# Out-projection of the last four token tiles by seven products per pair of blocks

## The chip, the core and the metric

The kernel runs on one core of one Trainium2 chip. The metric is the device time of one execution in microseconds (us). The engines are named as the profile names them: PE (matrix multiply), PEld (its weight loads), DVE (VectorE), ACT (ScalarE), POOL (GpSimd), SP (SyncE, which here only issues DMAs). Line numbers such as L800 are those of the kernel before; where the changed kernel is meant, the text says so.

## What is computed

Linear attention with a decay per head over 4 batches, 8 heads, 768 tokens and 64 channels a head, then a feed-forward part with a gate that is the cosine of the hidden value itself. Inputs and output are float32.

```python
for b in range(nb):                       # blocks of 64 tokens, per batch and head
    intra = (qb @ kb.T * Dmask) @ vb
    out[b] = intra + (qb * lam_pow) @ kv_state
    kv_state = lam_block * kv_state + (kb * rev_pow).T @ vb
x = out as (3072 tokens, 512)
h = x @ w_in                              # 512 x 2048
g = h * cos(h)
y = g @ w_out                             # 2048 x 512
```

## The kernel before

The 3072 tokens are 24 blocks of 128. `TILES = [4, 2, 2, 2, 2, 4, 4, 4]` groups the blocks into eight tiles of the feed-forward part. Attention works on pairs of blocks (pair `pr` is blocks 2 pr and 2 pr + 1 of the order of `where`).

**Attention.** q, k and v of a pair are loaded by SP (L260). From pair 3 on POOL prepares them (`qk` L351 and L355, `v_s` L359: two q, two k, two v a pair), and SP transposes `qk` by DMA (`qkT`, L387). The load of q of the next pair is queued behind these transposes, so the loads of a pair wait, over SP, for POOL's work on the pair before. An attention part on PE is values of pair `pr` (L491), scores of pair `pr + 1` (L429), its state update (L441), then the carried part of pair `pr` (L491, L523). Ahead of the carried part PE waits for a tiny DVE copy (`spare`, L508), here called the marker. DVE masks the scores (`s_m`, L434) and adds up the state (`sum`, L447); ACT casts the state (`S`, L451) and copies the result into `xT` (L531; L540 to L548 for two of the pairs).

**Hidden part.** For each of 16 slices f of 128 columns of `w_in`, four matmuls (one per quarter of 512 channels) write one PSUM bank `ps_h` (L753); ACT takes the cosine into `cos` (L759), DVE multiplies into `g` (L765, the gate). In tiles of two blocks a matmul has 256 columns, in tiles of four 512.

**Out-projection.** For each block, 16 matmuls of 512 columns accumulate `g` times `w_out_sb` in one bank `ps_f` (L800). ACT copies the bank to `o_sb` (L816), SP stores it (L823, L825). The very last block is split into 384 and 128 columns, whose second part ACT copies and stores.

**What sets the order.** A planner (`Planner.order`) runs a list schedule over tasks with costs written by hand and emits each engine's instructions in the order of the planned starts. An engine then goes through its own list strictly; what it waits for is set by the data. PE is filled with out-projection matmuls of the tile before while attention and hidden matmuls have to wait. `HELD = (10,) * 12` holds the stores of the first twelve blocks back until the transposes of pair 10 are issued. Buffers go round by tag (`BUFS`): `o_held` has 12 buffers, taken in turn by the early q and k of the first blocks, by four slices of `w_out` that are loaded plainly (`w_f`) and by the outputs.

```python
h = pl.add("PE", MM(n, 4), ..., hidden, pr, banks=1)
a = pl.add("ACT", 0.21 + n * 0.000833, [h], cosine, pr, get="cos")
d = pl.add("DVE", 0.12 + n * 0.00104, [a] + ..., gated, pr)
```

## Time and profile before

| what | before |
|---|---|
| median of 3 runs | 202.6 us (202.12 to 202.65) |
| profiled execution, first to last instruction | 200.7 us |
| clock granted to PE | 1.000 |
| instructions | 5731 |
| out-projection matmuls (L800) in the trace | 380, of 400 weight loads |
| hidden matmuls (L753) in the trace | 525, of 532 weight loads |
| DMA traffic | 34.46 MB, mean 172 GB/s |

The profiled execution leaves a span, from its first to its last instruction, and no separate device time; the runs' median is 1.9 us above it. A matmul's own duration in a row is its latency through a pipeline; its pace is found by dividing the length of a run of them by their count. Groups of rows read: line, engine, operation, output and inputs, shapes, count, then busy us, mean ns, and idle time before them with what ended it. A row of a timeline has start and length in us. In rows of the chain of waits the length is the part of the chain that the group holds. Rows of the windows have the stretch, its length, then for PE, PEld, DVE, ACT and POOL the busy us and the number of instructions, then PE's clock, DMA share and GB/s.

### The profile page before, as it was taken

The numbers are of one execution on the slowest core, as the hardware profiler recorded it, in microseconds if no ns is written. First come the engines' busy times: TensorE is split into PE (matmuls) and PEld (weight loads), VectorE is DVE, ScalarE is ACT, GpSimd is POOL, SyncE is SP. The second block draws the span as 40 slices with busy tenths as digits, with TensorE's granted clock in tenths as the row PEclk, the third lists the DMA queues.
The fourth block names the chain that finished last, engine by engine and source line by source line (L and its number), as shares of the span: only waits on it lengthen the run. The fifth ranks groups of instructions, "written<-read, shape, count | busy, mean of one in ns | idle before, by whom it ended". The sixth has DMA issues, their size and how long they took to land.

```text
span 200.7 us, 5731 instructions
## 1 busy us (share of the span) xinstructions
PE 192.9 (96%) x2380; PEld 110.2 (55%) x2407; DVE 112.1 (56%) x211; ACT 117.1 (58%) x223; POOL 64.9 (32%) x86
## 2 busy tenths in 40 slices
PE   8899999999999999999999999999999999999993
PEld 2466444648758647858755454544445444444452
DVE  2978772448848816956745679565445453444001
ACT  5878771329769527939555878486356465344120
POOL 5893002284373645472636570006400000000000
DMA  5999999999899999998999997999611010111112
GB/s 163 303 191 202 205 196 239 289 221 177 203 218 214 184 241 201 214 213 184 191 207 220 245 206 183 318 314 223 162 56 54 3 52 6 49 52 52 52 63 97
DMA packets 96668, 34.46 MB, mean 172 GB/s; under 512 B 84738, under 2 KB 93186, under 8 KB 96642
## 3 DMA queue, kind: packets, MB, share of 16 engines
q1 hardware_dynamic: 89664, 29.83, 66.6%
q0 software_dynamic: 6832, 4.20, 14.5%
q8 instruction: 19, 0.31, 0.7%
q10 hardware_dynamic: 146, 0.07, 0.1%
q14 instruction: 7, 0.06, 0.1%
HBM read 27.26 MB, written 6.29 MB: 167 GB/s over the span
## 4 chain that ended last, share of the span: by engine, by line
PE 89%; DMA 6%; issue 1%; SPq 1%; POOL 1%; ACT 0%; POOLq 0%
PE ps_f L800 41%; PE ps_h L753 41%; DMA sp_f<-in_k_dram 3%; DMA w_in_sb<-in_moe_w_in_dram 3%; PE ps_o L491 2%; PE ps_o L523 2%; PE ps_kv L441 2%; PE ps_s L429 1%; SPq L260 1%; POOL k_sp L614 1%; PE ps_t L381 0%; PE ps_kv L718 0%; PE ps_x L491 0%; ACT o_sb L816 0%; POOLq L614 0%
## 5 line engine op out<-in xcount | busy, mean ns | idle before, releaser
L765 DVE TENSOR_TENSOR g<-ps_h,cos 128x256 bf16<-128x256 f32 (+1 forms) x133 | 70.6, 543 | 41.4 <-ACT cos L759 39.7
L800 PE MATMUL ps_f<-w_out_sb,g 128*128 128x512 bf16 (+2 forms) x380 | 87.6, 370 | 2.2 <-issue 1.6
L753 PE MATMUL ps_h<-xT,w_in_sb 128*128 128x256 bf16 (+1 forms) x525 | 88.8, 319 | 0.5 <-issue 0.2
L759 ACT ACTIVATE cos<-ps_h,halfpi 128x256 f32<-128x256 f32 (+1 forms) x133 | 72.0, 570 | 28.9 <-PE ps_h L753 28.3
L753 PEld LDWEIGHTS <-w_in_sb 128*128 128x128 bf16 x532 | 51.4, 98 | 32.9 <-DMA w_in_sb<-in_moe_w_in_dram 0.4
L800 PEld LDWEIGHTS <-g 128*128 128x128 bf16 x400 | 37.6, 98 | 40.4
L351 POOL TENSOR_TENSOR qk<-q_f,q_scale 128x512 bf16<-128x512 f32 x19 | 19.4, 1042 | 54.2 <-DMA q_f<-in_q_dram 54.2
L816 ACT COPY o_sb<-ps_f 128x512 f32<-128x512 f32 (+1 forms) x24 | 13.7, 574 | 22.6 <-PE ps_f L800 19.6
L359 POOL TENSOR_TENSOR v_s<-v_f,v_scale 128x512 bf16<-128x512 f32 x19 | 19.6, 1043 | 9.2 <-DMA v_f<-in_v_dram 5.4
L531 ACT CAST xT<-ps_o 128x512 bf16<-128x512 f32 x15 | 8.1, 589 | 13.6 <-PE ps_o L523 11.2
L434 DVE TENSOR_TENSOR s_m<-ps_s,mask 128x512 bf16<-128x512 f32 x20 | 12.9, 685 | 2.5 <-PE ps_s L429 2.0
L355 POOL CAST qk<-k_f 128x512 bf16<-128x512 f32 x18 | 11.0, 612 | 7.8 <-DMA k_f<-in_k_dram 7.8
L447 DVE TENSOR_TENSOR sum<-sum,ps_kv 128x512 f32<-128x512 f32 x15 | 10.2, 682 | 0.7
L451 ACT CAST S<-sum 128x512 bf16<-128x512 f32 x15 | 9.1, 618 | 1.0 <-DVE sum L447 0.9
L508 DVE COPY spare<-ps_o 1x1 f32<-1x1 f32 x8 | 1.2, 156 | 14.6 <-PE ps_o L491 14.6
L816 DVE COPY o_sb<-ps_f 128x384 f32<-128x384 f32 x1 | 0.6, 558 | 11.6 <-PE ps_f L800 11.6
L491 PEld LDWEIGHTS <-v_s 64*64 64x64 bf16 x320 | 4.2, 106 | 4.4 <-issue 4.0
L491 PE MATMUL ps_o<-s_m,v_s 64*64 64x64 bf16 x288 | 5.9, 197 | 0.0
L638 DVE TENSOR_TENSOR s_m_sp<-ps_s,mask_sp 128x512 bf16<-128x512 f32 x8 | 5.1, 685 | 1.3 <-PE ps_s L633 1.3
L892 PE MATMUL ps_idle<-const-float32-1.0 128*128 128x512 f32 (+1 forms) x6 | 4.8, 902 | 0.8 <-PEq L954 0.8
L523 PE MATMUL ps_o<-qkT,S 64*64 64x64 bf16 x304 | 5.0, 195 | 0.0
L441 PE MATMUL ps_kv<-v_s,qk 64*64 64x64 bf16 x288 | 4.8, 195 | 0.0
(77 smaller groups left out, 83.9 us busy)
## 6 DMA issues: line engine op xcount, KB each, us to landing
q_f<-in_q_dram SPq DMA_DIRECT2D x20, 256.0 KB, 3.9
k_f<-in_k_dram SPq DMA_DIRECT2D x20, 256.0 KB, 4.5
v_f<-in_v_dram SPq DMA_DIRECT2D x20, 256.0 KB, 4.5
out_dram<-o_sb SPq DMA_DIRECT2D x19, 256.0 KB, 2.8
w_out_sb<-in_moe_w_out_dram POOLq DMA_DIRECT2D x3, 512.0 KB, 13.6
sp_f<-in_q_dram SPq DMA_DIRECT2D x2, 512.0 KB, 4.9
sp_f<-in_k_dram SPq DMA_DIRECT2D x2, 512.0 KB, 5.4
w_in_sb<-in_moe_w_in_dram POOLq DMA_DIRECT2D x2, 512.0 KB, 9.1
```

Of the source, the lines that this page charges most:

```text
L351: return vec[e].tensor_mul(new_qk()[:, 0, :, s], live.pop(("q_f", 2 * pr + s)), q_scale[:, c, :].unsqueeze(2).to_broadcast([P, H, D]))
L355: return (nc.scalar.copy if early else nc.gpsimd.tensor_copy)(new_qk()[:, 1, :, s], live.pop(("k_f", 2 * pr + s)))
L359: return vec[e].tensor_mul(live["v_s", 2 * pr + s], live.pop(("v_f", 2 * pr + s)), v_scale[:, c, :].unsqueeze(2).to_broadcast([P, H, D]))
L434: return nc.vector.tensor_mul(t, live["s", pr][s], mask.unsqueeze(1).to_broadcast([P, H, D]))
L447: return nc.vector.tensor_add(new, live["sum", pr, 0] if half else live["sum", pr - 1, 1], live["kv", pr][half])
L451: return nc.scalar.copy(new_S(pr, half), live["sum", pr, half])
L491: yield lambda h=h: nc.tensor.matmul(o[halves[h % 2], h // 2], lhsT=live["v_s", n0 + s][m, h, :], rhs=live["s_m", n0 + s][m, h, :], start= ...
L753: return [nc.tensor.matmul(t[:, :n], lhsT=w_in_sb[:, kd, f * P:(f + 1) * P], rhs=live["xT", i][:, kd, at], start=(kd == 0), stop=(kd == KD ...
L759: nc.scalar.activation(c[:, :n], live["h", i, f, at.start][:, :n], AF.Sin, bias=halfpi)
L765: return nc.vector.tensor_mul(live["g", i][:, f, at], live.pop(("h", i, f, at.start))[:, :n], live.pop(("c", i, f, at.start))[:, :n])
L800: return [nc.tensor.matmul(live["f", i, j, piece][:, :width], lhsT=live["g", i][:, f, j * P:(j + 1) * P], rhs=w_out_sb[:, f, part], start= ...
L816: return (nc.scalar.copy if eng == "ACT" else nc.vector.tensor_copy)(o[:, :width], live["f", i, j, piece][:, :width])
```

## The change

**Seven products.** In tiles 4 to 7 (`FAST`, 2, 4, 4 and 4 blocks) the out-projection takes two blocks at a time. The two blocks are the rows of a 2 x 2 block matrix A, the halves of the 2048 hidden columns its columns; `w_out` is a 2 x 2 block matrix B of halves of rows and of columns. Strassen's scheme forms the four quarters of the result from seven products instead of eight. A product is 8 matmuls of 256 columns, in two groups (g) of four. On the left stand sums of quarters of `g`: 5, 2 and 1 are new tiles `cmb`, 7 and 6 overwrite quarters of `g`, 3 and 4 use `g` as it is. DVE forms them (ten instructions a tile, five for each g; each has 512 elements in tile 4 and 1024 in the others, both operands bf16 in SBUF). On the right stand sums of quarters of `w_out`, formed once: three new tiles by six DVE instructions, and two sums written in place into `w_out_sb` by four POOL instructions, after the last plain projection. The in-place sums belong to products 6 and 7.

Products 5 and 2 fill a bank A, 1 a bank B, 3 and 4 a bank C. ACT copies A to `SA`, DVE forms `E` = B - A in two halves and the first outputs o1 = C + A; then 7 and 6 are added onto C and DVE forms the second outputs o2 = C + E. So product 7 has to wait for o1. Each output tile goes to two stores of 256 columns. The last pair's o2 is formed in two halves, the last of which ACT stores.

**Slices that share a bank.** In tiles of two blocks, slices f and f + 8 write the halves of one bank, so ACT and DVE work on 512 columns eight times instead of 256 sixteen times. Tiles of four take their slices in the order 0, 8, 1, 9 and so on.

**Homes.** The buffers are laid out anew: 4 instead of 6 for each of q, k and v, one tag `o` of 11 buffers for all outputs, new tags for `cmb`, `SA` and `E`; the early scores and values share their space with the three weight sums. The planner frees an engine a little earlier (`TAIL`).

```diff
+FAST = [4, 5, 6, 7]
+WSUM = [["DVE"] * 3 + ["POOL"] * 2, ["DVE"] * 3 + ["POOL"] * 2]
+SEQ = [[(n, (g,)) for g, x in enumerate(("52341", "34521")) for n in x] + [(n, (0, 1)) for n in "76"], [(n, (0, 1)) for n in "5234176"]]
...
+    TAIL = {"ACT": 0.1, "DVE": 0.09, "POOL": 0.05}
...
-            free[t.eng] = t.end
+            free[t.eng] = t.end - self.TAIL.get(t.eng, 0.0)
...
-    BUFS = {"ld": 6, "qk": 3, "v_s": 6, "qkT": 3, "s_m": 4, "cos": 3, "o_sb": 3, "o_held": 12}
+    BUFS = {"ld": 4, "qk": 3, "v_s": 6, "qkT": 3, "s_m": 4, "cos": 3, "o": 11, "cmb": 2, "SA": 2, "E": 2}
...
-    span_v = [consts.tile([P, H, 2, D], BF16, name=f"v_sp{x}") for x in range(SPANS)]
+    span_s = [consts.tile([P, 2, NP, 2, P], BF16, tag="wide", bufs=3, name=f"s_m_sp{x}") for x in range(SPANS)]
+    span_vs = consts.tile([P, SPANS, H, 2, D], BF16, tag="wide", bufs=3, name="v_sp")
+    span_v = [span_vs[:, x] for x in range(SPANS)]
...
+    def add_w_sums():
+        low, high = slice(0, HM), slice(HM, DM)
+        def fresh(name):
+            if name not in W:
+                W[name] = consts.tile([P, HF, HM], BF16, tag="wide", bufs=3, name=f"w_{name}")
+            return W[name]
+        def two(_, name, g, e):
+            f, z = slice(QF * g, QF * g + QF), slice(HF + QF * g, HF + QF * g + QF)
+            b11, b12, b21, b22 = (w_out_sb[:, x, y] for x in (f, z) for y in (low, high))
+            v = nc.vector if e == "DVE" else nc.gpsimd
+            if name == "11+22":
+                return v.tensor_add(fresh(name)[:, f], b11, b22)
+            if name == "12-22":
+                return v.tensor_sub(fresh(name)[:, f], b12, b22)
+            if name == "21-11":
+                return v.tensor_sub(fresh(name)[:, f], b21, b11)
+            if name == "11+12":
+                return v.tensor_add(b12, b11, b12)
+            return v.tensor_add(b21, b21, b22)
+        on = {"DVE": 0.69, "POOL": 2.1}
+        for g in range(2):
+            loaded = [w_t["out", 0], w_t["out", 2]] if g == 0 else [w_t["out", 1]] + w_last
+            for k, name in enumerate(("11+22", "12-22", "21-11")):
+                e = WSUM[g][k]
+                w_sum[name, g] = [pl.add(e, on[e], loaded + (wide_free if name == "21-11" else []), partial(two, name=name, g=g, e=e), begins[FAST[0]] + 3.0 + 2.0 * g + 0.4 * k)]
+        for g in range(2):
+            for k, (name, others) in enumerate((("11+12", ("12-22",)), ("21+22", ("21-11",)))):
+                e = WSUM[g][3 + k]
+                w_sum[name, g] = [pl.add(e, on[e], [closed[0]] + [t for o in others for t in w_sum[o, g]], partial(two, name=name, g=g, e=e), begins[FAST[0] + 1] + 0.4 * k + 0.2 * g)]
+    def held(n):
+        return [T[HELD[n], 1].issue] if n < len(HELD) else []
...
+        if i == 0:
+            groups = [([f], b, (f + b[0] / 4 * SPLIT) / KF) for f in range(KF) for b in ([(0, 2), (2, 4)] if f < SPLIT else [(0, nb)])]
+        elif nb == 4:
+            groups = [([f], (0, nb), (2 * (f % HF) + f // HF) / KF) for x in range(HF) for f in (x, x + HF)]
+        else:
+            groups = [([x, x + HF], (0, nb), 2 * x / KF) for x in range(HF)]
+        for fs, (b0, b1), frac in groups:
+            pr = begins[i] + frac * unit[i]
+            at = slice(b0 * P, b1 * P)
+            n = (b1 - b0) * P
+            k, key = len(fs), (i, fs[0], b0)
...
+            def hidden(task, fs=fs, at=at, n=n, key=key):
+                t = bank(task.bank[0], [P, 4 * P], F32, "ps_h")
+                live["h", key] = t
+                return [nc.tensor.matmul(t[:, x * n:(x + 1) * n], lhsT=w_in_sb[:, kd, f * P:(f + 1) * P],
+                                         rhs=live["xT", i][:, kd, at], start=(kd == 0), stop=(kd == KD - 1))
+                        for x, f in enumerate(fs) for kd in range(KD)]
...
-            cuts = [0, 3 * DM // 4, DM] if last else [0, DM]
...
+            for f0, nf in [(0, 4), (4, 4), (8, 4), (12, 2), (14, 2)] if i == 0 else [(0, 4), (8, 4), (4, 4), (12, 4)]:
...
+        def combine(_, name, g):
+            a11, a12, a21, a22 = (side(x, y, g) for x in range(2) for y in range(2))
+            if ("cmb", i, g) not in live:
+                live["cmb", i, g] = work.tile([P, 3, QF, np_, P], BF16, tag="cmb", bufs=BUFS["cmb"], name="cmb")
+            c = live["cmb", i, g]
+            if name == "5":
+                return nc.vector.tensor_add(c[:, P5], a11, a12)
+            if name == "2":
+                return nc.vector.tensor_add(c[:, P2], a21, a22)
+            if name == "1":
+                return nc.vector.tensor_add(c[:, P1], a11, a22)
+            if name == "7":
+                return nc.vector.tensor_sub(a12, a12, a22)
+            return nc.vector.tensor_sub(a21, a21, a11)
+        for g in range(2):
+            ready = [t for f in range(QF * g, QF * g + QF) for t in gate[f] + gate[f + HF]]
+            head = None
+            for k, name in enumerate("52176"):
+                t = pl.add("DVE", 0.15 + np_ * QF * P / 1920.0, ready + ([head] if head else []), partial(combine, name=name, g=g),
+                           begins[i] + (0.55 + 0.06 * k + 0.45 * g) * unit[i], get=None if head else "cmb")
+                head = head or t
+                sums[name, g] = [t]
+            sums["head", g] = head
+            sums["3", g] = sums["4", g] = ready
...
+        plan_of = {"5": ("A", 0, "22"), "2": ("A", 1, "11"), "1": ("B", 0, "11+22"), "3": ("C", 0, "12-22"),
+                   "4": ("C", 1, "21-11"), "7": ("C", 1, "21+22"), "6": ("C", 0, "11+12")}
+        def left(name, f, p):
+            j = 2 * p
+            own = lambda x, y: live["g", i][:, f + HF * y, (j + x) * P:(j + x + 1) * P]
+            if name in "125":
+                return live["cmb", i, f // QF][:, {"1": P1, "2": P2, "5": P5}[name], f % QF, p]
+            return own(*{"3": (0, 0), "4": (1, 1), "6": (1, 0), "7": (0, 1)}[name])
...
+            for name, gs in SEQ[min(p, 1)]:
+                to, half, what = plan_of[name]
+                for g in gs:
+                    k += 1
+                    def product(task, name=name, g=g, p=p, to=to, half=half, what=what):
+                        if (name, g) in (("5", 0), ("1", 0), ("3", 0)):
+                            live["f", i, p, to] = bank(task.bank[0], [P, 2, HM], F32, "ps_f")
+                        t = live["f", i, p, to][:, half]
+                        return [nc.tensor.matmul(t, lhsT=left(name, f, p), rhs=right(what, f),
+                                                 start=(f == 0 and name in "513"), stop=(f == HF - 1), skip_group_check=True)
+                                for f in range(QF * g, QF * g + QF)]
+                    opens = (name, g) in (("5", 0), ("1", 0), ("3", 0))
+                    t = pl.add("PE", MM(HM, QF), sums[name, g] + w_sum.get((what, g), []) + [before] + ([done["o1"]] if name == "7" else []) + ([passed.get("4")] if (name, g) == ("5", 0) else []) + ([passed.get("6")] if (name, g) == ("3", 0) else []),
+                               product, begins[i + 1] + (p + k / 14) * nxt / np_, banks=1 if opens else 0)
...
+                if "sa" not in done and full("5") and full("2"):
+                    def copy_out(_, p=p):
+                        live["SA", i, p] = work.tile([P, 2, HM], F32, tag="SA", bufs=BUFS["SA"], name="SA")
+                        return nc.scalar.copy(live["SA", i, p], live["f", i, p, "A"])
+                    done["sa"] = pl.add("ACT", 0.6, [done["5"], done["2"]], copy_out, begins[i + 1] + (p + 0.2) * nxt / np_, get="SA")
+                    heads["A"].bank_frees = [[done["sa"]]]
+                if "e" not in done and "sa" in done and full("1"):
+                    def differ(_, half, p=p):
+                        if half == 0:
+                            live["E", i, p] = work.tile([P, 2, HM], F32, tag="E", bufs=BUFS["E"], name="E")
+                        return nc.vector.tensor_sub(live["E", i, p][:, half], live["f", i, p, "B"][:, 0], live["SA", i, p][:, 1 - half])
+                    e0 = pl.add("DVE", 0.43, [done["1"], done["sa"]], partial(differ, half=0), begins[i + 1] + (p + 0.4) * nxt / np_, get="E")
+                    done["e"] = pl.add("DVE", 0.43, [e0], partial(differ, half=1), begins[i + 1] + (p + 0.4) * nxt / np_)
+                    heads["B"].bank_frees = [[done["e"]]]
+                if "o1" not in done and "sa" in done and full("3") and full("4"):
+                    def first_out(_, p=p):
+                        o = live["o1", i, p] = work.tile([P, 2, HM], F32, tag="o", bufs=BUFS["o"], name="o_sb")
+                        return nc.vector.tensor_add(o, live["f", i, p, "C"], live["SA", i, p])
+                    done["o1"] = pl.add("DVE", 0.69, [done["3"], done["4"], done["sa"]], first_out, begins[i + 1] + (p + 0.6) * nxt / np_, get="o")
...
+            def second_out(_, half, p=p):
+                if ("o2", i, p) not in live:
+                    live["o2", i, p] = work.tile([P, 2, HM], F32, tag="o", bufs=BUFS["o"], name="o_sb")
+                h = slice(0, 2) if half is None else half
+                return nc.vector.tensor_add(live["o2", i, p][:, h], live["f", i, p, "C"][:, h], live["E", i, p][:, h])
...
+            if last:
+                x = pl.add("DVE", 0.43, [done["7"], done["e"]], partial(second_out, half=1), pr, get="o")
+                y = pl.add("DVE", 0.43, [done["6"], x], partial(second_out, half=0), pr)
+                x.frees = [dma("SP", 0.6, 0.7, partial(store_second, half=1), n0 + 2 * p + 9, [x], ordered=False)[1],
+                           dma("ACT", 0.6, 0.7, partial(store_second, half=0), n0 + 2 * p + 9, [y], ordered=False)[1]]
...
+            else:
+                x = pl.add("DVE", 0.69, [done["7"], done["6"], done["e"]], partial(second_out, half=None), pr, get="o")
+                x.frees = [dma("SP", 0.95, 1.3, partial(store_second, half=None), n0 + 2 * p + 9, [x] + held(n0 + 2 * p), ordered=False)[1]]
```

How the order moves, at three places.

PE, at the end of the last attention part ahead of tile 5's hidden matmuls. Before (`ps_o` is attention, `ps_f` out-projection, `ps_h` hidden), the last of eight 512-column matmuls stand ahead of the hidden ones:

```order
L800 LDWEIGHTS g
L800 MATMUL ps_f<-w_out_sb,g 128x512
L800 LDWEIGHTS g
L800 MATMUL ps_f<-w_out_sb,g 128x512
L753 LDWEIGHTS w_in_sb
L753 MATMUL ps_h<-xT,w_in_sb 128x512
```

Now, from the end of the attention part on:

```order
L529 MATMUL ps_o<-qkT,S_2192 64x64
L969 LDWEIGHTS g
L969 MATMUL ps_f<-w_out_sb,g 128x256
L969 LDWEIGHTS g
L969 MATMUL ps_f<-w_out_sb,g 128x256
L969 LDWEIGHTS g
L969 MATMUL ps_f<-w_out_sb,g 128x256
L969 LDWEIGHTS g
L969 MATMUL ps_f<-w_out_sb,g 128x256
L816 LDWEIGHTS w_in_sb
L816 MATMUL ps_h<-xT,w_in_sb 128x512
```

Four matmuls of 256 columns (half of product 7) stand where eight of 512 stood.

DVE, around the marker of the same attention part. Before, at the end of tile 4:

```order
L765 TENSOR_TENSOR g<-ps_h,cos 128x256 x3
L508 COPY spare<-ps_o 1x1
L434 TENSOR_TENSOR s_m<-ps_s,mask 128x512 x2
L447 TENSOR_TENSOR sum_2499<-sum_2292,ps_kv 128x512
L447 TENSOR_TENSOR sum_2502<-sum_2499,ps_kv 128x512
```

Now (`cmb` and `g<-g` are the combinations, in the order 5, 2, 1, 7, 6; the `o_sb` is o1):

```order
L828 TENSOR_TENSOR g<-ps_h,cos 128x2x256
L914 TENSOR_TENSOR cmb<-g 128x512
L916 TENSOR_TENSOR cmb<-g 128x512
L918 TENSOR_TENSOR cmb<-g 128x512
L920 TENSOR_TENSOR g<-g 128x4x128
L921 TENSOR_TENSOR g<-g 128x4x128
L993 TENSOR_TENSOR E<-ps_f,SA 128x256
L1000 TENSOR_TENSOR o_sb<-ps_f,SA 128x512
L514 COPY spare<-ps_o 1x1
L993 TENSOR_TENSOR E<-ps_f,SA 128x256
```

Seven instructions of the out-projection have come between the last gate and the marker.

POOL, over pairs 8 and 9 (8 is the first three rows). Before:

```order
L351 TENSOR_TENSOR qk<-q_f,q_scale 128x8x64 x2
L355 CAST qk<-k_f 128x8x64 x2
L359 TENSOR_TENSOR v_s<-v_f,v_scale 128x512 x2
L351 TENSOR_TENSOR qk<-q_f,q_scale 128x8x64 x2
L355 CAST qk<-k_f 128x8x64 x2
L359 TENSOR_TENSOR v_s<-v_f,v_scale 128x512 x2
```

Now, from the first v_s of pair 8 on:

```order
L365 TENSOR_TENSOR v_s<-v_f,v_scale 128x512
L772 TENSOR_TENSOR w_out_sb<-w_out_sb 128x4x256
L365 TENSOR_TENSOR v_s<-v_f,v_scale 128x512
L772 TENSOR_TENSOR w_out_sb<-w_out_sb 128x4x256
L773 TENSOR_TENSOR w_out_sb<-w_out_sb 128x4x256 x2
L357 TENSOR_TENSOR qk<-q_f,q_scale 128x8x64
L365 TENSOR_TENSOR v_s<-v_f,v_scale 128x512
L361 CAST qk<-k_f 128x8x64
L357 TENSOR_TENSOR qk<-q_f,q_scale 128x8x64
L361 CAST qk<-k_f 128x8x64
L365 TENSOR_TENSOR v_s<-v_f,v_scale 128x512
```

The four in-place sums stand ahead of pair 9, and in pair 9 a v_s and a k have moved ahead of the second q.

More of the change, by code (lines that the diff above doesn't have):

```diff
@@ L737, in add_ffn @@
+    def held(n):
+        return [T[HELD[n], 1].issue] if n < len(HELD) else []
     def add_ffn(i):
+        nonlocal closing
         nb, n0 = TILES[i], first[i]
+        np_ = nb // 2
         cols = nb * P
         gate = {}
[L742 to L780 removed]
@@ new lines, in project_plain, with project_out, store_out @@
+            o_last[i] = store
+            def project_out(_, j=j):
+                o = live["o", i, j] = work.tile([P, DM], F32, tag="o", bufs=BUFS["o"], name="o_sb")
+                return nc.scalar.copy(o, live["f", i, j])
+            def store_out(_, j=j):
+                b, c = where(n0 + j)
+                r0 = b * S + c * P
+                if n0 + j >= 2 * SPANS:
+                    nc.sync.dma_start(out=out[r0:r0 + P], in_=live["o", i, j])
+                    return
+                for s, h in enumerate(halves):
+                    nc.sync.dma_start(out=out[r0 + s:r0 + P:2, :], in_=live["o", i, j][h])
```

207 lines of the change are left out of this document (122 added, 85 removed).

## The prediction

> **What bounds the kernel now.** I read the page's busy shares first, then the chain that ended last, then TensorE's own waits.
>
> ```profile
> span 200.7 us, 5731 instructions
> PE 192.9 (96%) x2380; PEld 110.2 (55%) x2407; DVE 112.1 (56%) x211; ACT 117.1 (58%) x223; POOL 64.9 (32%) x86
> ...
> PE 89%; DMA 6%; issue 1%; SPq 1%; POOL 1%; ACT 0%; POOLq 0%
> ```
>
> TensorE (PE) is busy for 96% of the span and is 89% of the chain. The other compute engines are busy for 58% or less. So two things move the time: the matmul work itself, and any moment in which PE has to wait. The waits of PE are these:
>
> ```profile
> PE ps_f L800 <- issue: 1.6, 10, 0.2
> PE ps_idle L892 <- PEq L954: 0.8, 1, 0.8
> PE ps_t L622 <- DVE k_sp L614: 0.3, 1, 0.3
> ```
>
> After the first 16 us PE waits for no other engine. A change that removes matmul work is paid in full here, unless the helper work that it adds makes PE wait.
>
> **What is removed.** The chain in order of time gives the true pace of the matmuls (a single row's duration is latency, so I divide a run by its count).
>
> ```profile
> 77.68 6.99 PE ps_h L753 x64
> ...
> 101.34 5.18 PE ps_f L800 x24
> ...
> 183.76 6.69 PE ps_f L800 x31
> 190.45 0.05 issue
> 190.50 7.12 PE ps_f L800 x48
> 197.65 0.27 ACT o_sb L816
> ```
>
> A matmul of 512 columns takes 5.18/24 = 0.2158 us, one of 256 columns 6.99/64 = 0.1092 us. The 256-column run loads a new stationary block for each matmul, as the products will, so 0.1092 holds for them. Two token blocks cost 32 x 0.2158 = 6.91 us before; seven products of 8 matmuls cost 56 x 0.1092 = 6.12 us now, 0.79 less, and there are seven pairs: 5.5 us. The last tile took 197.65 - 183.76 = 13.9 us with its split last block, 0.07 more than 64 x 0.2158, so **5.6 us** of PE work goes. The first four tiles keep theirs.
>
> In the Trainium skill, "TensorE: Matmul & The Clock Gate", section "Back-to-back issue gap", a sustained stream with weight loads is put at some 131 ns for 512 columns. By that rule a pair would cost 32 x 0.131 = 4.2 us before, and seven products could only lose, by 1.9 us a pair. The measured 0.2158 us decides against it here.
>
> **What is added, and what hides it.** The nearest rows:
>
> ```profile
> L765 DVE TENSOR_TENSOR g<-ps_h,cos 128x512 bf16<-128x512 f32 x59 | 40.5, 691 | 31.7 <-ACT cos L759 31.2
> L765 DVE TENSOR_TENSOR g<-ps_h,cos 128x256 bf16<-128x256 f32 x74 | 30.3, 424 | 9.8 <-ACT cos L759 8.5 <-DMA v_f<-in_v_dram 0.7
> L816 ACT COPY o_sb<-ps_f 128x512 f32<-128x512 f32 x23 | 13.4, 587 | 19.7 <-PE ps_f L800 16.7 <-remote 2.9
> L759 ACT ACTIVATE cos<-ps_h,halfpi 128x512 f32<-128x512 f32 x59 | 40.4, 687 | 24.1 <-PE ps_h L753 23.6
> L384 DVE COPY qkT<-ps_t 128x1024 bf16<-128x1024 bf16 x2 | 1.4, 692 | 3.3 <-PE ps_t L381 3.3
> L359 POOL TENSOR_TENSOR v_s<-v_f,v_scale 128x512 bf16<-128x512 f32 x19 | 19.6, 1043 | 9.2 <-DMA v_f<-in_v_dram 5.4 <-PE ps_h L753 2.4 <-PE ps_kv L441 0.9
> 131.60:159.60 28.00, 27.58 (x294) 13.34 (x296) 13.97 (x23) 15.68 (x27) 5.31 (x6) 1.00 0.49 129
> ```
>
> No row adds two bf16 operands on VectorE (DVE). A combination of 1024 bf16 elements lies between the 1024-element bf16 copy, 0.69, and the 512-element rate doubled, 0.42 + 2 x 0.27 = 0.96 to 1.22 (256 elements more cost 0.27). I take 0.69, the row of equal size and type, and keep 1.22 as a rival. So a tile of four blocks adds ten combinations (6.9), four E of 256 (1.7) and four outputs of 512 (2.8): 11.4 us of DVE. The last row is a stage of 28.0 us with two attention parts; its DVE goes from 13.97 to 25.4, and the PE stage shrinks by 1.6 to 26.4. Queued DVE work overlaps by some 0.08 a piece (two s_m of 0.685 take 1.29 together), so about 22.7 of 26.4: DVE fits, but **with little room**. ACT loses four output copies and gains two SA copies, so it is no worry.
>
> In tiles 1 to 4 sixteen evictions of 256 become eight of 512: ACT and DVE lose 16 x 0.424 - 8 x 0.691 = 1.3 us a tile. PE did not wait for them, so this brings nothing.
>
> Now the places where PE can wait. I set the end of tile 4's hidden matmuls at t0 = 101.3, where PE stood before too. From there the order has 40 products (4.37 us), the attention part that ends pair 7, four products, and the hidden matmuls of tile 5.
>
> ```profile
> 106.52 0.25 PE ps_o L491 x16
> ...
> 107.34 0.16 PE ps_o L491 x16
> ...
> 107.84 0.16 issue
> 108.00 1.67 PE ps_f L800 x7
> 109.68 9.06 PE ps_h L753 x42
> ...
> 106.82 0.16 DVE L508 COPY spare<-ps_o 1x1 f32<-1x1 f32 x1 [3.08 <-PE ps_o L491]
> 107.98 1.07 ACT L531 CAST xT<-ps_o 128x512 bf16<-128x512 f32 x2 [1.70 <-PE ps_o L523]
> ```
>
> 1. *Cover after an attention part.* Its xT copies end 109.05 - 107.84 = 1.2 us after its last matmul, and with a hop the hidden matmuls can start at 1.26. Before, eight projection matmuls covered this. Now four products of 0.11 stand there, 0.44 + 0.16 = 0.60: PE waits **0.7 us**. Those products also need the third in-place weight sum on GpSimd (POOL); see 3.
>
> 2. *The marker `spare` behind E and o1.* Tile 4's second-half combinations start when its last gate is done, at t0 + 0.05 + 0.69 + 0.69 = 1.4. They have 512 elements, at the doubled rate as long as 256 single ones (0.42), so 5, 2 and 1 are ready at 1.9, 2.3 and 2.7; PE wants them at 28, 32 and 36 products, 3.06, 3.50 and 3.93. SA follows product 2: 3.93 + 0.05 + 0.59 = 4.57; then E 4.99, o1 5.65, the marker 5.75. PE reaches the matmuls behind the marker at 4.37 + 0.83 (107.34 - 106.52 in the old order) = 5.2: **0.55 us**. Bounds: nothing, if E starts earlier, and 1.0, if each hop takes 0.1 more.
>
> 3. *POOL, loads, stores.* Each in-place sum is two operands of 1024: 2 x 1.04 = 2.08. They start when tile 3's last projection ends, about 100.5, with one v_s between them.
>
> ```profile
> 104.58 2.04 POOL L351 TENSOR_TENSOR qk<-q_f,q_scale 128x512 bf16<-128x512 f32 x2 [2.94 <-DMA q_f<-in_q_dram]
> ...
> 106.65 3.43 SPq L387 DMA_TRANSPOSE qkT<-qk  x2
> 110.14 1.20 SPq L260 DMA_DIRECT2D q_f<-in_q_dram  x2
> ...
> 116.29 3.05 SPq L387 DMA_TRANSPOSE qkT<-qk  x2
> 119.43 6.53 SPq L823 DMA_DIRECT2D out_dram<-o_sb  x8
> ...
> out_dram<-o_sb SPq DMA_DIRECT2D x8, 128.0 KB, 3.3
> ...
> qkT<-qk SPq DMA_TRANSPOSE x18, 4.5
> ```
>
> The sums end at 100.5 + 4 x 2.08 + 1.04 = 109.9, so pair 9's preparation begins 5.3 us late and, with v_s and k between its two q, its transposes some 6 to 7 us late. On SP everything behind them shifts: pair 10's loads to 116, its transposes to 122.4, the first stores from 119.4 to 125.5. The transposes land 4.5 after their issue, by about 129. The scores need them at 131: hidden tile 5 from 108.3, 60 of its matmuls and 12 products to 122.6, an attention part of 1.5, four matmuls and 56 products (0.9 + 6.1). So they are in time by 2. The outputs are held until then, and o2 of tile 4 takes the buffer of block 0, which is free at 125.5 + 0.8 + 3.3 = 129.6; o1 behind it needs block 1, two stores of 0.82 later, at 131.2. DVE is there at 129.8 (five combinations behind the last gate) and 130.8, so o1 ends at 131.9 and the marker follows at 132.0, where PE wants it at 131.8: **0.2 us**. Bounds: nothing if the chain is 0.2 us faster, 2 if it is 2 slower, since all of it then passes through.
>
> 4. *The start.* Six weight sums stand on DVE between 30 and 46 us, 0.69 each, where DVE is busy 6.50 of 15.50 us:
>
> ```profile
> 30.50:46.00 15.50, 15.08 (x232) 8.26 (x235) 6.50 (x12) 4.48 (x8) 6.46 (x8) 1.00 1.02 252
> ```
>
> Two of them stand ahead of S and xT; the projection matmuls ahead of these were put at 12 and 8 instead of 10 and 6, which covers nearly all: **0.3 us**, from 0 to 1.
>
> 5. *Product 7 waits for o1, since both use one bank.* The cover is product 1, 8 x 0.109 = 0.87, against 0.69 + two hops of 0.05 to 0.1: from nothing to 0.1 a pair, together **0.4 us**.
>
> 6. *The end.*
>
> ```profile
> out_dram<-o_sb SPq DMA_DIRECT2D x1, 192.0 KB, 1.9
> ...
> out_dram<-o_sb ACTq DMA_DIRECT2D x1, 64.0 KB, 1.6
> ```
>
> The last eviction is 256 wide on DVE, 0.42 instead of 0.27, and its store has 128 KB instead of 64, between 1.6 and 1.9: **0.3 us**.
>
> The sum is 200.7 - 5.6 + 0.7 + 0.55 + 0.2 + 0.3 + 0.4 + 0.3 = 197.6 us of span. The median of the runs, 202.6, is 1.9 above the profiled span; with that the forecast is **199.5 us**.
>
> **The rivals.**
>
> *Nothing waits.* The planned order hides 1 to 5: 200.7 - 5.6 + 0.3 + 1.9 = 197.3. For it speaks DVE's idle time; against it that the covers above were counted and are short.
>
> *Slower: DVE and POOL in turns.* The combinations read both operands from SBUF, and so do POOL's sums. If one engine holds the other off for a whole instruction, then around t0 each combination waits for a sum of 2.08. Combination 2 comes at 104.0 + 2.08 + 0.42 = 106.5 instead of before 104.8 (1.7 late), combination 1 another 2.5 later where 0.44 was allowed (2.1 late), and one more of 2.1 stands ahead of the marker: some 6 us on top of the forecast, **205.5**. It gives a slower kernel once it delays PE by 3.7 us, which two such turns do. For it: four sums and a v_s follow each other without a gap exactly there. Against it: no row of before shows a DVE instruction with two SBUF operands beside a POOL one, so the trace is silent. The Trainium skill, "SBUF — State Buffer", section "SBUF: two separate sides", says exactly this: the shared port pair is an exclusive lock for the whole instruction. No row here shows it.
>
> *Combinations at half rate.* With 1.22 each, DVE needs 22.7 + 10 x 0.53 = 28.0 of 26.4. Combination 2 of the second half is then 0.7 late, 1 another 0.6, and o1 and the marker behind 7 and 6 another 1: 2.3 for each of three tiles and 1 for tile 4, some 7.9 on top of the forecast, **207.4**. The Trainium skill, "VectorE: DVE Perf Modes", section on the perf-mode tier table, gives bf16 tensor_tensor in SBUF a doubled rate, which speaks against this rival; no row here shows it.
>
> *The chain of step 3 is 3 us longer* (transposes or buffers late): 202.5, the same as before.
>
> *The products don't run at 0.109*, for instance 0.12 because a weight load takes 0.098 of it: 392 x 0.011 = 4.3 more, 203.8. The run of 64 above speaks against it.
>
> **How the numbers follow.** Forecast 0.45, nothing waits 0.17, turns 0.17, chain 0.10, half rate 0.07, slow products 0.04. The forecast's own range is 198 to 201.5. To leave out no more than two in ten, the range reaches from the case without waits to the case of turns: 197.0 to 205.5. A measurement here tells 0.3% apart, that is below 202.0 or above 203.2. Faster: 0.45 + 0.17 + a third of the chain = 0.65; slower: turns, half rate and slow products without their mild ends, 0.28 - 0.03 = 0.25; same: the rest, 0.10.
>
> **What would show it.** Right: the chain has runs of 256-column products at 0.109 us, hidden tile 5 starts 0.5 to 0.9 us after product 7, combinations of 1024 take 0.69. Wrong: PE's waits name DVE combinations for over 2 us (turns or half rate; the start-to-start of combinations beside POOL's sums tells which), or the scores of pair 10 wait for qkT, or o_sb for a store.

## The result and the profile after

From here on a line number is that of the kernel whose row is shown. Executions that come out over 1.5% longer than the fastest of the same kernel are left out of the ratios; their times are given where there were any.

| | before | changed |
|---|---|---|
| median of the runs | 202.53 us (4 runs) | 211.19 us (4 runs, 210.5 to 211.91) |
| ratio to before, 95% interval | | 1.0427 (1.0408 to 1.0447) |
| span of the profiled execution | 200.7 us | 209.4 us (of 211.08) |

The kernel became **slower by 4.3%**. The forecast was 199.5 us and the range ended at 205.5. The measured span is 11.8 us longer than the forecast one of 197.6. The page of the changed kernel first (span, busy shares, the clock granted to PE in 40 slices, the chain by engine):

```profile
span 209.4 us, 6043 instructions
...
PE 192.7 (92%) x2536; PEld 127.4 (61%) x2559; DVE 155.2 (74%) x253; ACT 108.7 (52%) x184; POOL 75.7 (36%) x90
...
PEclk9999999999999999999969699999999999999998
...
PE 79%; DVE 11%; DMA 3%; issue 2%; ACT 1%; SPq 1%; POOL 1%; POOLq 0%; ACTq 0%
```

Two things are new. DVE, which the chain of before does not name, is 11% of it; and the clock row has two dents, in the slices from 104.7 to 109.9 and from 115.2 to 120.4 us (before, the clock was 1.000). What PE waited for (total, times, longest):

```profile
PE ps_o L497 <- DVE spare L514: 5.8, 2, 4.3
...
PE ps_h L816 <- DVE xT L537: 1.1, 1, 1.1
...
PE ps_kv L447 <- DVE g L828: 0.7, 1, 0.7
```

All of these name DVE, and so does one of 0.5 for o2 (o_sb). The longest is the marker in tile 4's hidden part. The timelines of DVE and of POOL ahead of it (start, length):

```profile
96.77 0.42 DVE L914 TENSOR_TENSOR cmb<-g 128x512 bf16<-128x512 bf16 x1
97.11 0.68 DVE L828 TENSOR_TENSOR g<-ps_h,cos 128x512 bf16<-128x512 f32 x1
97.71 1.15 DVE L916 TENSOR_TENSOR cmb<-g 128x512 bf16<-128x512 bf16 x1
...
99.38 1.74 DVE L918 TENSOR_TENSOR cmb<-g 128x512 bf16<-128x512 bf16 x1
101.05 1.26 DVE L920 TENSOR_TENSOR g<-g 128x512 bf16<-128x512 bf16 x1
102.23 2.33 DVE L921 TENSOR_TENSOR g<-g 128x512 bf16<-128x512 bf16 x1
104.59 0.16 DVE L514 COPY spare<-ps_o 1x1 f32<-1x1 f32 x1
```

```profile
97.54 1.04 POOL L365 TENSOR_TENSOR v_s<-v_f,v_scale 128x512 bf16<-128x512 f32 x1 [1.55 <-DMA v_f<-in_v_dram]
98.53 2.30 POOL L772 TENSOR_TENSOR w_out_sb<-w_out_sb 128x1024 bf16<-128x1024 bf16 x1
100.81 1.22 POOL L365 TENSOR_TENSOR v_s<-v_f,v_scale 128x512 bf16<-128x512 f32 x1
101.99 2.29 POOL L772 TENSOR_TENSOR w_out_sb<-w_out_sb 128x1024 bf16<-128x1024 bf16 x1
104.24 2.30 POOL L773 TENSOR_TENSOR w_out_sb<-w_out_sb 128x1024 bf16<-128x1024 bf16 x1
```

Read them side by side. The combination at 96.77, with POOL idle, takes 0.42 us. The next four, of the same size, take 1.15, 1.74, 1.26 and 2.33, and each of these four ends within 0.3 us of the end of a POOL instruction (98.58, 100.83, 102.03, 104.28). The gates (L828), which read one operand from PSUM, keep their 0.68. Two of these lines in the groups, by shape:

```profile
L918 DVE TENSOR_TENSOR cmb<-g 128x1024 bf16<-128x1024 bf16 x6 | 4.1, 683 | 0.0
...
L921 DVE TENSOR_TENSOR g<-g 128x512 bf16<-128x512 bf16 x2 | 3.6, 1794 | 0.0
L918 DVE TENSOR_TENSOR cmb<-g 128x512 bf16<-128x512 bf16 x2 | 3.0, 1500 | 0.0
```

In tiles 5 to 7, where POOL is idle for most of the time, a combination of 1024 elements takes 0.68. In tile 4, beside POOL, those of half the size take 1.5 and 1.8 in the mean of two. The theory with which the experiments began was therefore the rival "DVE and POOL in turns"; its rivals were combinations that are slow by themselves, and a cost that comes with the rest of the change (order, homes, shared banks).

### The profile page after: what moved, and what is told of

Its sections match the earlier page's. It is cut to its first block, busy times and chain, and to the rows that moved or that the text cites. A ratio compares the mean times of both kernels' runs of the same rounds, so it can differ in the third digit from the quotient of the medians.

```text
span 209.4 us, 6043 instructions
## 1 busy us (share of the span) xinstructions
PE 192.7 (92%) x2536; PEld 127.4 (61%) x2559; DVE 155.2 (74%) x253; ACT 108.7 (52%) x184; POOL 75.7 (36%) x90
## 4 chain that ended last, share of the span: by engine, by line
PE 79%; DVE 11%; DMA 3%; issue 2%; ACT 1%; SPq 1%; POOL 1%; POOLq 0%; ACTq 0%
PE ps_h L816 39%; PE ps_f L969 18%; PE ps_f L863 15%; DMA sp_f<-in_k_dram 3%; DVE g L828 2%; DVE cmb L918 1%; PE ps_o L497 1%; PE ps_o L529 1%; SPq L266 1%; PE ps_kv L447 1%; DVE g L921 1%; DVE g L920 1%; DVE cmb L916 1%; DVE cmb L914 1%; PE ps_s L435 1%
## 5 line engine op out<-in xcount | busy, mean ns | idle before, releaser
L828 DVE TENSOR_TENSOR g<-ps_h,cos 128x512 bf16<-128x512 f32 (+1 forms) x101 | 66.2, 663 | 26.5 <-ACT cos L822 25.6
L822 ACT ACTIVATE cos<-ps_h,halfpi 128x512 f32<-128x512 f32 (+1 forms) x101 | 66.8, 666 | 33.4 <-PE ps_h L816 32.3
L816 PEld LDWEIGHTS <-w_in_sb 128*128 128x128 bf16 x532 | 52.3, 99 | 32.0 <-issue 1.8
L863 PE MATMUL ps_f<-w_out_sb,g 128*128 128x512 bf16 x146 | 35.3, 382 | 1.5 <-issue 1.1
L969 PEld LDWEIGHTS <-cmb 128*128 128x128 bf16 x168 | 16.6, 100 | 4.0 <-issue 0.7
L969 PE MATMUL ps_f<-w_out_sb,g 128*128 128x256 bf16 x112 | 15.3, 277 | 0.7 <-DVE o_sb L1020 0.5
L969 PE MATMUL ps_f<-w_out_sb,cmb 128*128 128x256 bf16 x112 | 14.5, 279 | 0.0
L361 POOL CAST qk<-k_f 128x512 bf16<-128x512 f32 x18 | 11.8, 658 | 4.2 <-DMA k_f<-in_k_dram 4.2
L986 ACT COPY SA<-ps_f 128x512 f32<-128x512 f32 x7 | 4.1, 585 | 16.0 <-PE ps_f L969 16.0
L880 ACT COPY o_sb<-ps_f 128x512 f32<-128x512 f32 x10 | 5.7, 589 | 7.3 <-PE ps_f L863 7.3
L969 PE MATMUL ps_f<-w_11+22_579,cmb 128*128 128x256 bf16 x56 | 8.2, 272 | 0.5 <-issue 0.5
```

Of the source, the lines that this page charges most:

```text
L361: return (nc.scalar.copy if early else nc.gpsimd.tensor_copy)(new_qk()[:, 1, :, s], live.pop(("k_f", 2 * pr + s)))
L816: return [nc.tensor.matmul(t[:, x * n:(x + 1) * n], lhsT=w_in_sb[:, kd, f * P:(f + 1) * P], rhs=live["xT", i][:, kd, at], start=(kd == 0), ...
L822: nc.scalar.activation(c[:, :m], live["h", key][:, :m], AF.Sin, bias=halfpi)
L828: return nc.vector.tensor_mul(g, x(live.pop(("h", key))), x(live.pop(("c", key))))
L863: return [nc.tensor.matmul(live["f", i, j], lhsT=live["g", i][:, f, j * P:(j + 1) * P], rhs=w_out_sb[:, f], start=(f == 0), stop=(f == KF ...
L969: return [nc.tensor.matmul(t, lhsT=left(name, f, p), rhs=right(what, f), start=(f == 0 and name in "513"), stop=(f == HF - 1), skip_group_ ...
```

## The experiments

**1. The two engines alone and side by side** (e1_pairs). A kernel with only DVE and POOL instructions on tiles in SBUF and one in PSUM, first one engine at a time, then both at once. It leaves out all of the computation. The stages, in short form (the names stand for the instructions, L for their lines; the last two stages are left out here):

```python
stage((add512, 6), none)                                    # L52: DVE alone, 512 bf16
stage(none, (lambda: nc.gpsimd.tensor_add(p1, b1, b2), 3))  # L55: POOL alone, 1024 bf16
stage((add512_pair, 12), (pool_add, 4))                     # L57 / L58: both
stage((mul_with_psum, 12), (pool_add, 4))                   # L59 / L60
stage((add512_pair, 12), (pool_memset, 8))                  # L61 / L62
stage((copy1024, 12), (pool_add, 4))                        # L63 / L64
...
```

> The feed-forward and attention parts are left out: this runs only VectorE and GpSimd instructions, alone and side by side, on the chip. Theory 1 (turns): a VectorE instruction with two SBUF operands and a GpSimd instruction that reads SBUF hold each other off for a whole instruction. Then adds of 512 bf16 alone start some 0.34 us apart; beside GpSimd adds of about 2.1 us each the first four or so take 2 us and more, and GpSimd's adds start some 2.4 apart instead of 2.1; beside GpSimd memsets, or when VectorE reads one operand from PSUM, nothing changes (0.34 and 0.60). Theory 2 (half rate): bf16 adds are simply slow, so a 512 add takes 0.65 or more when it is alone too, and the same beside GpSimd. Theory 3 (sharing): both slow down by some fraction, beside memsets too.

Groups by line (count, then busy us and mean ns of one):

```profile
L57 DVE TENSOR_TENSOR d<-a,a 128x512 bf16<-128x512 bf16 x12 | 12.3, 1023 | 9.1 <-POOL p L56 8.7
...
L58 POOL TENSOR_TENSOR p<-b,b 128x1024 bf16<-128x1024 bf16 x4 | 8.9, 2219 | 0.3
...
L59 DVE TENSOR_TENSOR d<-ps,f 128x512 bf16<-128x512 f32 x12 | 8.3, 691 | 0.5
...
L61 DVE TENSOR_TENSOR d<-a,a 128x512 bf16<-128x512 bf16 x12 | 5.1, 426 | 0.5
...
L54 DVE TENSOR_TENSOR d<-a,a 128x1024 bf16<-128x1024 bf16 x6 | 4.2, 692 | 0.2
L52 DVE TENSOR_TENSOR d<-a,a 128x512 bf16<-128x512 bf16 x6 | 2.6, 426 | 0.3
```

And the single instructions of L57 (shortest, median, longest in ns):

```profile
L57 DVE TENSOR_TENSOR d<-a,a x12: 424/426/2221, 24.4 to 36.6; 128x512 bf16<-128x512 bf16 x12
```

Alone, 512 elements take 0.426 and 1024 take 0.692 us, so the price of the prediction was right for DVE alone and half rate is out. Beside POOL's sums the mean is 1.023, but no single one is near it. POOL's four sums run from 24.4 to 33.6 us; the four DVE sums that start at 24.9, 27.1, 29.4 and 31.6 us take 2.22 each, as long as one POOL sum (2.219 in the mean), and the other eight, nearly all behind POOL's last sum, take 0.43. One DVE sum goes by for each POOL sum: that is waiting in turns for whole instructions, not a slowdown by a fraction. With an operand in PSUM (L59, 0.691, as in the gates of the kernel before), or beside memsets, which read nothing (L61, 0.426), nothing changes. One number of the expectation was off: alone the DVE sums start 0.46 apart, not 0.34. The last stage, with two f32 inputs on each engine (L67 1.398, L68 1.619 in the mean), has no counterpart alone and is not used.

**2. POOL's four sums as memsets** (e2_sums_as_memsets). Each in-place sum becomes two memsets of the same tile, so POOL is at work for about as long (2 x 0.95 for 2.1) and reads nothing. These sums are left out of what is computed.

```diff
-            if name == "11+12":
-                return v.tensor_add(b12, b11, b12)
-            return v.tensor_add(b21, b21, b22)
+            to = b12 if name == "11+12" else b21
+            nc.gpsimd.memset(to, 0.01)
+            return nc.gpsimd.memset(to, 0.02)
```

> The four in-place weight sums on GpSimd are left out: two memsets each stand in their place, on the same tiles, in the same order, so that GpSimd writes but reads nothing there. Theory 1 (turns): the combinations 1, 7 and 6 of tile 4's first half, 1.74, 1.26 and 2.33 us in the changed kernel, fall towards 0.42 except where one meets a v_s; the marker comes some 3 us earlier and the span falls from 209.4 to 205 to 206.5. Theory 4 (GpSimd is late, whatever it does): the memsets take about as long as the sums, so span and marker stay within 0.7 us of the changed kernel's.

Measured 205.71 us (one run), 5.5 less than the changed kernel; its span of 204.0 lies below the 205 to 206.5 that were expected. DVE's timeline at the same place, and two rows of POOL's, which is busy with memsets from 98.71 to 104.5:

```profile
97.60 1.07 DVE L916 TENSOR_TENSOR cmb<-g 128x512 bf16<-128x512 bf16 x1
...
99.19 0.41 DVE L918 TENSOR_TENSOR cmb<-g 128x512 bf16<-128x512 bf16 x1
...
99.86 0.41 DVE L921 TENSOR_TENSOR g<-g 128x512 bf16<-128x512 bf16 x1
100.30 0.16 DVE L514 COPY spare<-ps_o 1x1 f32<-1x1 f32 x1
```

```profile
98.71 0.95 POOL L772 MEMSET w_out_sb<- 128x1024 bf16 x1 [0.32 <-PE ps_f L863]
99.72 0.95 POOL L773 MEMSET w_out_sb<- 128x1024 bf16 x1
```

The three combinations from 99.19 on are back at 0.41; the one left long, at 97.60, ends beside a v_s of POOL that reads SBUF. The marker comes at 100.30 instead of 104.59; PE's wait for it falls from 4.3 to 0.2, and both markers together from 5.8 to 1.8. The 1.6 that are left are at the second marker: from 104.4 to 110.6 POOL prepares q, k and v of the next pair, which read SBUF, and four of tile 4's second five combinations still take 0.82 to 1.27 there. So POOL's reading, not POOL's being busy, and not the combinations themselves, made the great wait.

**3. The four sums on DVE** (e3_sums_on_vector).

```diff
-WSUM = [["DVE"] * 3 + ["POOL"] * 2, ["DVE"] * 3 + ["POOL"] * 2]
+WSUM = [["DVE"] * 5, ["DVE"] * 5]
```

> The four in-place weight sums are moved from GpSimd to VectorE, nothing else. Theory 1: the collisions with sums go, those with the preparation of pairs 8 and 9 stay; 204.5 to 208 us, so between before and the changed kernel. Theory 4 (GpSimd's lateness): pair 9 is prepared 8 us earlier, so most of the loss goes: 199 to 203. Theory 2 (half rate, VectorE too full): VectorE gets 2.8 us more work ahead of product 7, 211 to 214.

Measured 206.57 and 206.12 us, ratio to before 1.0191 (1.017 to 1.0211); two more executions took 209.33 and 209.86. Nothing of the computation is left out here, and some 5 us come back: inside the range of theory 1. Two of the four sums met POOL's two v_s of 105.70 to 108.24 us instead:

```profile
105.82 2.98 DVE L773 TENSOR_TENSOR w_out_sb<-w_out_sb 128x1024 bf16<-128x1024 bf16 x2
```

That is 2.98 for two that take 0.69 each alone. The next combination is done only at 109.13, and PE stands for 2.7 us ahead of the product that needs it (109.23). The cost moves with the work as long as POOL prepares attention there.

**4. No products at all** (e4_no_products): what the other parts of the change cost.

```diff
-FAST = [4, 5, 6, 7]
+FAST = []
```

> No tile uses the products (the list of tiles is empty), so there are no combinations and no weight sums; the shared banks of small tiles, the new homes and the new order of slices stay. If the products and their helpers are to blame: 202 to 204 us (the last block is no longer split, up to 0.7 more at the end). If the shared banks or the fewer buffers cost: 205 or more.

Measured 204.56 us, ratio 1.0096 (1.0079 to 1.0113). That is between what either side expected: 2 us over the kernel before without any product. (Experiment 9 puts about 0.8 of them down to the undivided last block, which the changed kernel does not have.) The profiled execution took 205.71 us, 1.2 more than the median, and had one wait of 1.5 us for a load of `w_in`. The chain of this kernel has a large piece of ACT ahead of tile 3's hidden part:

```profile
78.23 1.07 ACT xT L537 x2
```

I took it for 1.1 us of waiting. PE's own waits say otherwise:

```profile
PE ps_kv L447 <- DVE g L828: 0.7, 1, 0.7
PE ps_h L816 <- ACT xT L537: 0.2, 1, 0.2
```

Four projection matmuls run beside the copy, so PE stood for only 0.2 us. The chain shows what released what, not how long the engine stood.

**5 and 6. Fewer tiles** (e5_last_two_tiles, e6_last_three_tiles): products only where POOL has little or nothing left to do, all weight sums on DVE.

```diff
-FAST = [4, 5, 6, 7]
+FAST = [6, 7]
```

> Seven products in tiles 6 and 7 alone, all ten weight sums on DVE late in the program, where POOL has ended its work. Theory 1 (turns between DVE and POOL, and a late order in the rest): no combination and no weight sum meets POOL, so each takes 0.68 to 0.70. Four pairs save 4 x 0.79 = 3.2 us against the kernel without products (204.56), the eight projection matmuls ahead of tile 3's or 4's hidden part are back behind the attention part (1.1 less there), the end and o1 cost 0.6: 200.9 us, 200 to 201.8. Rival (DVE has no room for 30 combinations and 10 weight sums in the last 45 us, POOL or not): 203 to 206, PE waits on DVE there. Rival (the 2 us of the kernel without products lie in the slices that share a bank, not in two waits): 201.9.

> Seven products in tiles 5 to 7, all weight sums on DVE. Two more pairs save 1.6 us against tiles 6 and 7 alone, the cover of four products ahead of a hidden part costs 0.7 once, and the weight sums now stand beside POOL's work on pairs 9 and 10 in tile 5's hidden part, where DVE has slack. Theory 1: 199.5 to 201.0, no PE wait on a combination over 0.5. Rival (DVE has no room, POOL or not): 204 to 207.

In the second of the two kernels FAST is [5, 6, 7]. Measured 203.0 us, ratio 1.0029 (1.0013 to 1.0044), and 203.67 us, ratio 1.0051 (1.0033 to 1.0068): the one is 2.1 above the 200.9 expected, the other 2.7 above the end of its range. In the first kernel combinations take 0.68 us each and no wait of PE names one; in the second PE waited for gates that stand among combinations and sums (2.1 us ahead of two state updates), so part of its rival held: DVE has little room there. What was missed in both is the start. Its chain in the run with two tiles:

```profile
42.82 0.69 DVE w_11+22_579 L766
...
44.23 0.73 DVE w_12-22_587 L768
44.96 1.45 DVE w_21-11_731 L770
46.41 0.61 DVE xT L537
47.06 7.16 PE ps_h L816 x64
```

The weight sums stand ahead of S (left out above) and xT, the third (which took 1.11 in the mean of two there) holds 1.45 us of the chain, and tile 1 starts at 47.06 (before: 45.76). The chain of the changed kernel has the last two sums there as well, and it starts tile 1 at 47.41.

**7 and 8. A wait put into the kernel before** (e7_before_wait_4us, e8_before_wait_1us): is the dent in the clock a consequence of the wait, or of the short products? At the marker ahead of tile 5, behind a first copy, 32 (or 10) memsets on DVE:

```diff
+            if pr == 7:
+                nc.vector.tensor_copy(spare[D:D + 1, 0:1], live["o", n0][D:D + 1, NP - 1, D:D + 1])
+                for _ in range(32):
+                    nc.vector.memset(spare, 0.0)
```

> The kernel before with 32 extra DVE memsets of 112 elements between a first marker copy and the marker that PE waits for, at the attention part ahead of tile 5: PE stands for some 4 us, nothing else changes. Theory (a long wait of PE is followed by some 10 us at a lower granted clock, whatever stands behind it): the PE clock falls to 0.6 to 0.9 for some us behind the wait, and the time grows by the wait plus 1.5 to 3: 208 to 210. Rival (the clock fell because of the short products, not of the wait): clock 1.00 everywhere, 202.5 + the wait, 206 to 207.

> As the run with 32 memsets, with 10: PE stands for some 1.3 us. If the clock falls only behind long waits: clock 1.00, 203.5 to 204. If any wait does it: 204.5 to 205.5 with a dip in the clock.

The memsets took longer than planned, so PE stood 7.5 us in the one and 2.2 in the other. Measured 212.14 us, ratio 1.0478 (1.0464 to 1.0491), and 205.59 us, ratio 1.0152 (1.0129 to 1.0175). Windows of the kernel with 32 (stretch, length, busy us of PE, PEld, DVE, ACT, POOL, then PE's clock):

```profile
108.00:112.00 4.00, 0.00 (x0) 0.00 (x0) 2.54 (x17) 0.00 (x0) 1.22 (x2) 1.00 1.15 167
112.00:114.00 2.00, 0.00 (x0) 0.00 (x0) 1.22 (x9) 0.00 (x0) 1.04 (x1) 0.58 1.18 264
...
116.00:118.00 2.00, 1.69 (x4) 0.64 (x6) 1.66 (x3) 1.61 (x3) 1.40 (x3) 0.50 0.97 222
118.00:120.00 2.00, 2.00 (x8) 0.84 (x7) 0.00 (x0) 0.53 (x1) 0.98 (x1) 0.71 0.74 166
120.00:124.00 4.00, 4.00 (x21) 1.79 (x19) 2.41 (x4) 3.41 (x7) 0.00 (x0) 1.00 0.89 207
```

PE's last matmul ahead of the wait ends at 107.6 and its next one starts at 115.1. If the clock is either 1.00 or 0.50, the 0.58 means half clock from 112.3 on and the 0.71 full clock from 119.2 on: it falls some 5 us into the wait and comes back about 4 us after PE works again. Tile 5's hidden part starts 9.7 us later than before (119.39, not 109.68) for a wait of 7.5: 2.2 on top, within the 1.5 to 3 of the theory. With 2.2 us of waiting the clock of the profiled execution is 1.00. (The median of these runs is 3.1 us above before; one of the four shows a clock of 0.992, and the 0.9 us beyond the wait are not explained.) So the dent follows a long wait, with no product in the kernel.

**9. No products, with the order of before** (e9_no_products_order): two chunks of projection are made to wait for the attention part behind which they stood before.

```diff
+        for c, x in (((2, 1, 4), 4),((4, 1, 4), 7),):
+            if i == c[0] + 1:
+                chunk[c].deps.append(v12[x])
         add_ffn(i)
```

> The kernel without products, with two chunks of four projection matmuls (the third chunk of the last block of tiles 2 and 4) made to wait for the carried matmuls of the attention part that follows. PE's order then has eight projection matmuls instead of four ahead of the hidden parts of tiles 3 and 5, and 44 and 20 hidden matmuls around the next attention part, as in the kernel before. Theory (the 2 us over the kernel before are two waits of PE that the new order uncovered: xT 1.1, kv bank 1.0): 202.3 to 202.8, both waits gone. Rival (they lie in the slices that share a bank or in the new homes): 204.0 to 204.6, as without this edit.

Measured 204.72 us, ratio 1.0111 (1.009 to 1.0132). Three of the six runs were 3 us longer than their span, where it is 1.7 to 1.8 in the other kernels; by the spans (202.0 to 202.6, against 202.5 to 203.9 without the order) it gained some 0.4 us, so that expectation fell too. Its xT wait is gone, but it was worth 0.2; the wait for the kv bank stayed at 0.7, though the number of hidden matmuls around it was put back. Its span of 202.2 us in the profiled execution is 1.5 above that of before: 0.7 is this wait, and about 0.8 is the end, where the last block is no longer split (its last copy takes 0.58 instead of 0.27, and the store behind it is of 256 KB). The second does not exist in kernels with products in the last tile. What makes the kv wait, the new gates or the new banks, was not tried.

**10 and 11. Late weight sums and the order of before** (e10_two_tiles_order_late_sums, e11_three_tiles_order_late_sums). The six fresh sums wait for a late hidden matmul, on top of the edits of 9 and of 5 (or 6):

```diff
-... = [pl.add(e, on[e], loaded + (wide_free if name == "21-11" else []), ...
+... = [pl.add(e, on[e], loaded + [h_last[5]] + (wide_free if name == "21-11" else []), ...
```

> Seven products in tiles 6 and 7, all weight sums on DVE, the first six not before the last hidden matmul of tile 5 (about 127 us, where POOL ends), and the two chunks as in the run without products. Theory: the start is back (hidden part of tile 1 at 45.8 instead of 47.1), xT and kv waits are gone, no combination or sum meets POOL; against the run of the last two tiles (203.0) 1.3 + 0.9 + 0.7 less: 200.1, 199.7 to 200.7. Rival (ten weight sums between 127 and 160 us crowd DVE and PE waits for them): 201.5 to 203.

> The same with tiles 5 to 7; the first six sums not before the last hidden matmul of tile 4, so beside POOL's work on pairs 9 and 10. Two more pairs save 1.6 us, two attention parts with a product part and more DVE work cost some of it. Theory: 199.0 to 200.5. Rival (DVE has no room in tile 5's hidden part, since the sums meet POOL and take about 1 us each): 201 to 203, with PE waits on kv or a combination.

With two tiles: **201.47 us, ratio 0.9952 (0.9938 to 0.9966)**, 0.5% faster than the kernel before, though 0.8 above the upper end expected of 200.7. PE waits for no weight sum and no combination, so the rival of a crowded DVE did not come about; the 0.7 us for the kv bank, which the theory had called gone, are still there. Tile 1 starts at 45.83 again, and sums and combinations have the lengths that they have alone. (POOL's last preparation, 135 to 142 us, fell between them.)

```profile
L915 DVE TENSOR_TENSOR cmb<-g 128x1024 bf16<-128x1024 bf16 x4 | 2.7, 686 | 0.2 <-PE ps_f L970 0.2
...
L770 DVE TENSOR_TENSOR w_21-11_2714<-w_out_sb 128x1024 bf16<-128x1024 bf16 x2 | 1.4, 680 | 0.0
```

With three tiles (where the sums wait for h_last[4]): 204.05 us in the median of nine runs (202.51 to 206.04, two of them not in the ratio), ratio 1.0062 (1.0035 to 1.0088). The trace is that of the longest, 206.04. There the fresh sums stand beside POOL's work on pair 9, and are long (0.68 alone):

```profile
L770 DVE TENSOR_TENSOR w_21-11_2202<-w_out_sb 128x1024 bf16<-128x1024 bf16 x2 | 3.1, 1526 | 0.0
```

PE waits 2.2 us for the marker behind them and 1.4 for a mask ahead of a state update. The mechanism of that expectation's rival held; the time is above its 203.

## Why the prediction was wrong, by its steps

*What is removed: right.* The last run of products, with a wait of 0.2 us in it:

```profile
192.14 12.51 PE ps_f L969 x112
```

12.51 / 112 = 0.112 us each, against the 0.1092 of the sum; the rival of slow products (0.12) is out.

*"I take 0.69": right alone, and this is the step that failed.* The price came from rows whose input lies in PSUM (L765 and L384 of the kernel before); the sum used it for combinations, whose inputs all lie in SBUF, beside POOL. The run of the two engines shows that the one kind is not held up there (0.691) and that the other is (0.426 becomes 2.22). The same lack is in the price of POOL's sums (2.08; 2.11 alone, 2.30 here).

*Step 2, the marker, 0.55: it was 5.8.* The sum followed the second half of tile 4's combinations only. The first half stands ahead of an earlier marker, inside tile 4's hidden part. In turns with POOL it made PE wait 4.3 us there; with memsets on POOL that marker cost 0.2, and with the sums on DVE no wait for a marker is left. The second marker, the one that was costed, took 1.5: its five combinations took 0.82 to 1.29 each beside POOL's q, k and v, not 0.42.

*The clock, not in the sum.* Behind the 4.3 us wait, work that took 0.65 and 0.87 us at full clock took

```profile
105.41 1.19 PE ps_f L863 x3
106.60 1.72 PE ps_h L816 x8
```

The 8 matmuls alone lost 0.85. Put together in this way (each run of matmuls from 104.8 to 120 us against its length at full clock) it is some 3 us, an estimate from those rows. The second dent follows the 1.5 us at the second marker. That waits cost more than their length was shown in the kernel before (7.5 us of waiting, 9.7 of delay).

*Step 4, the start, 0.3: it was 1.65* (47.41 against 45.76), beyond its bound of 1.

```profile
42.88 1.41 DVE L766 TENSOR_TENSOR w_11+22_579<-w_out_sb 128x1024 bf16<-128x1024 bf16 x1
...
44.92 0.81 DVE L768 TENSOR_TENSOR w_12-22_587<-w_out_sb 128x1024 bf16<-128x1024 bf16 x1
45.66 1.09 DVE L770 TENSOR_TENSOR w_21-11_731<-w_out_sb 128x1024 bf16<-128x1024 bf16 x1
```

Three weight sums stand ahead of S and xT, not the two of the prediction, and beside POOL's q and k (42.7 to 46.2 us) they take 3.31 us instead of 3 x 0.69 = 2.07: the same step failed here. Moving them late brought tile 1 back to 45.83.

*Step 3, the chain over POOL, SP and the stores: right in time, without weight.* The first stores in SP's queue of the changed kernel:

```profile
126.68 1.83 SPq L889 DMA_DIRECT2D out_dram<-o_sb  x3
```

Forecast was 125.5. But PE reached that place some 11 us later than planned (142.4 against 131), and none of its waits names a transpose or a store.

*Steps 1, 5 and 6: right in size.* The xT cover left 0.2 of waiting behind its four products instead of 0.7, but by luck: they ran in the second dent and took about 0.4 longer than at full clock, at which some 0.6 would have been left; o1 and o2 made PE wait 0.7 (o_sb at two places, 0.2 and 0.5) instead of 0.4; from the last eviction to the end of the span it is 209.4 - 206.2 = 3.2 us, against 2.8 before.

In all: 1.35 more at the start, 5.25 more at the markers and some 3 by the clock make 9.6 of the 11.8 us. Of the other 2.2, the wait for the kv bank is 0.7, which the kernel without products has as well, and 0.5 is a wait ahead of 113.17 us for combination 1 of the second half; the rest is spread over small waits.

*The rivals.* "DVE and POOL in turns" was the mechanism. It had the chance 0.17 and a price of 6 us; the price left out the first marker, the start and the clock, and the range ended where that price did. That it comes near the 5.8 of the two markers is luck: it puts everything at the second one, which took 1.5. The argument against it was that the trace is silent. Silence is no evidence against, and the prediction itself had two arguments for it: four sums that follow each other exactly where the combinations stand, and a rule of the Trainium skill, "SBUF — State Buffer", section "SBUF: two separate sides", by which a DVE instruction with two SBUF inputs and a GpSimd one that reads SBUF exclude each other for a whole instruction. The runs agree with that rule: 2.22 us beside a sum of 2.22, four times in a row, and no change with PSUM or memsets. "Half rate" is refuted by 0.426 and 0.692 alone.

## What to carry to other kernels

Before work goes to an engine that looks idle, look at which neighbour runs at that time and where both read from: a DVE sum with both operands in SBUF cost 0.43 us alone and 2.2 beside a GpSimd sum, while an instruction with one operand in PSUM cost 0.69 in both cases. Follow every instruction that newly stands ahead of a marker or a copy for which TensorE waits, at each such place and not only at the last one, and count a wait of several us as more than its length, since the clock falls behind it. Where a change has good and bad stages, keep the good ones: the products gained 0.5% in the last two tiles alone, beside which GpSimd had hardly anything left to do.
